# Two rows of a planner's table of durations: VectorE's searches and replacements, and activations into PSUM

## The chip, the cores and the metric

One core of one Trainium2 chip. The time is that of one execution on the device in microseconds, from which the median of three runs is given. The engines are TensorE (PE, with its weight loads PEld), VectorE (DVE), ScalarE (ACT), GpSimd (POOL) and SyncE (SP, which here issues DMAs).

## The reference

Top-k attention, and behind it two MLPs. Softmax runs over the 32 largest scores of each row alone.

```
B, H, S, D = 4, 8, 576, 64
scores = q @ k.T / sqrt(D);  kth = 32nd largest of each row
scores = where(scores >= kth, scores, -1e9);  attn = softmax(scores);  x = attn @ v      # x: 2304 x 512
h = x @ w_in;   g = 0 | (h+1)^2/4 | h  (h <= -1, between, h >= 1);   x = g @ w_out       # 512 -> 2048 -> 512
h = relu(x @ w_in2);   out = (h*h) @ w_out2
```

## The kernel before, in words

The 2304 rows of tokens form 18 token tiles T of 128 rows, and each has 8 heads, so there are 144 tiles of scores t = 8T + j. T = 4 and T = 13 hold rows of two batches, and each of their tiles takes two heads with 64 rows each. One tile of scores goes through:

- `scores`: 4 matmuls (8 in T = 4 and 13) into one of two PSUM areas, `s0` for even and `s1` for odd tiles
- `topk_ops`: on DVE four searches (`max`, the 8 largest of 576) and between them three replacements (`match_replace`, which blots out the 8 that were found; on the chip a MATCH_VALUE_LOAD and a MATCH_REPLACE8). The first search and the first replacement read `s`, the others the SBUF copy `W`. Each needs the one before it
- `below_` and `exp` on ACT, `exp_bias` (`nb`) on POOL, `prob_hi` on ACT and `prob_lo` on POOL (`pc`, high and low half in F16), `prob_trans` by a DMA on SP (`pT`)
- `attend`: 14 or 28 matmuls of `pT` with `vst` into an accumulator that shares PSUM tiles with the areas of scores

`below_` of tile t is the last reader of its area, so the scores of tile t+2 wait for it. `attend` shares banks with the area of the other parity and waits for DVE's reads of it.

Beside this run the preparation of k, v and q (`v_prep`: scaling on POOL or DVE, high half on ACT, rest on POOL or DVE; `q_scale`: a square sum `junk_q` on ACT, then `sc_q` and more on DVE), the decoding and splitting of the weights into `wall` in the first 270 us or so, and the MLPs in groups n of 24 matmuls: `h_n` into PSUM, then `mlp_act` (`r`, and in the first MLP a third activation that writes back into the PSUM tile `h`), `mlp_gate` on DVE, `mlp_split` (`g` or `gr`, ACT and POOL), and `o`. The room `xhl` is there once and is shared by `junk_q`, `qhl`, `hl_x`, `hl_y`.

What sets the order: `Book.note` takes down every operation with what it depends on and a key (the step at which it is due, less an urgency). `Book.order` then plays all of them through with durations from `Book.costs`: each engine takes, of the operations whose inputs would be there by then, the one with the smallest key. What comes out is written as the program, one in-order queue for each engine, with semaphores. `costs` gives two numbers: for how long the engine is taken, and when the result is there. Gaps in PE's queue while the weights are decoded, as the planner sees them, are filled with matmuls of `ones` (PLAN "warm", 15 to 300 us of its own time). All rows of the profile have line 400, where the operations are issued.

Of the kernel before, what the change touches and what calls it, by code (L numbers as in the profile page):

```python
# [143 lines left out]
class Book:  # L144
# [107 lines left out]
    def costs(self, engine, method, args, kwargs, outs, ins):  # L252
        views = [v for v in outs + ins if v.elements() > 8]
        n = max((v.elements() for v in outs), default=0)
        wide = any(v.tile.ring.psum for v in views)
        aps = sum(isinstance(a, View) and a.elements() == 1 for a in (*args[2:], kwargs.get("bias"), kwargs.get("scale"), kwargs.get("accum_out")))
        if engine == "PE":
            c = n * (4 if args[2].ap.dtype is F32 else 1) / 2400.0 + 0.0024
            return c, c + 0.16
        if method == "dma_start_transpose":  # L260
            return (1.33 if n < 1100 else 1.41), n * 256 / 1000 / 165
        if method == "dma_start":
            v = (outs + ins)[0]
            return 0.6, 4 * v.elements() * v.ap.ap[0][1] / 1000 / (210 if outs and len(v.ap.ap) > 2 else 420)
        if engine == "DVE":
            if method == "max":
                return 0.68, 0.75
            if method == "match_replace":
                return 0.76, 0.85
            c = 0.07 + (n if method != "tensor_reduce" else 128) / 960 + (0.05 if n > 64 else 0.0)  # L270
            return c, c + 0.08
        if engine == "ACT":
            c = 0.155 + n / 1400 - (0.03 if wide else 0.0) + 0.09 * aps - (0.04 if n < 300 else 0.0)
            return c, c + 0.1
        if method == "memset":
            return 0.07, 0.07
        c = 0.14 + n / 522 if method == "tensor_tensor" else 0.14 + n / 940 + (0.08 * aps if n < 8 else 0.0)
        if any(v.ap.dtype is U16 for v in ins):
            c += 0.1
        return c, c  # L280
# [1218 lines left out]
```

## Time and profile before

| | us |
|---|---|
| median of 3 runs | 1068.32 (1068.06 to 1068.46) |
| the profiled execution | 1068.74 |
| its span, first to last instruction | 1067.0 |
| PE busy | 1000.5 |
| DVE busy | 915.3 |
| ACT busy | 847.4 |
| POOL busy | 673.1 |

The granted TensorE clock was 0.995 of full speed over the span. Busy times are sums over stages that differ; which engine ends a stage is read from stretches and from the gaps in front of instructions (in square brackets: how long the engine had been idle, and what released it).

### The profile page before, as it was taken

The numbers are of one execution on the slowest core, as the hardware profiler recorded it, in microseconds if no ns is written. First come the engines' busy times: TensorE is split into PE (matmuls) and PEld (weight loads), VectorE is DVE, ScalarE is ACT, GpSimd is POOL, SyncE is SP. The second block draws the span as 40 slices with busy tenths as digits, with TensorE's granted clock in tenths as the row PEclk, the third lists the DMA queues.
The fourth block names the chain that finished last, engine by engine and source line by source line (L and its number), as shares of the span: only waits on it lengthen the run. The fifth ranks groups of instructions, "written<-read, shape, count | busy, mean of one in ns | idle before, by whom it ended". The sixth has DMA issues, their size and how long they took to land.

```text
span 1067.0 us, 24296 instructions
## 1 busy us (share of the span) xinstructions
PE 1000.5 (94%) x8576; PEld 560.1 (52%) x8576; DVE 915.3 (86%) x2053; ACT 847.4 (79%) x1538; POOL 673.1 (63%) x1052
## 2 busy tenths in 40 slices
PE   4867889899889999999999999999999999999998
PEld 3744567666567544544544545444445445454443
DVE  5999999999999999999999999999999999991100
ACT  4778999999678898878988797987878887775542
POOL 4696989999667574648776564667674646553221
PEclk9989999999999999999999999999999999999999
DMA  9999886755766687879988778789767676764333
GB/s 251 319 312 235 218 214 141 141 123 99 136 115 121 128 157 139 158 135 155 185 135 143 120 139 159 136 154 169 150 131 130 108 136 114 123 107 92 75 59 66
DMA packets 433834, 158.11 MB, mean 148 GB/s; under 512 B 412208, under 2 KB 419376, under 8 KB 433712
## 3 DMA queue, kind: packets, MB, share of 16 engines
q1 hardware_dynamic: 433712, 156.56, 72.9%
q8 instruction: 67, 1.10, 0.4%
q14 instruction: 55, 0.45, 0.1%
HBM read 55.31 MB, written 4.72 MB: 56 GB/s over the span
## 4 chain that ended last, share of the span: by engine, by line
PE 66%; ACT 9%; DVE 7%; DMA 6%; POOL 6%; issue 4%; SPq 1%; POOLq 0%; ACTq 0%; DVEq 0%
PE h L400 28%; PE o L400 28%; PE s L400 9%; DVE m L400 2%; DVE W L400 2%; ACT wall L400 2%; ACT W L400 2%; POOL wall L400 2%; DMA l_q<-in_q_dram 2%; POOL pc L400 1%; DMA pT<-pc 1%; SPq L400 1%; ACT r L400 1%; DMA wall<-in_moe_w_in_dram 1%; DMA l_v<-in_v_dram 1%
## 5 line engine op out<-in xcount | busy, mean ns | idle before, releaser
L400 PE MATMUL o<-wall,g 128*128 128x512 f16 x1728 | 430.4, 379 | 9.8 <-POOL g L400 3.8
L400 DVE MAX8 m<-W 128x8 f32<-128x576 f32 x432 | 323.7, 755 | 5.6
L400 PEld LDWEIGHTS <-g 128*128 128x128 f16 x1728 | 159.6, 98 | 188.5 <-issue 6.2
L400 POOL TENSOR_TENSOR pc<-W,pc 128x64 f16<-128x64 f32 (+1 forms) x288 | 205.3, 734 | 76.0 <-ACT pc L400 65.8
L400 POOL TENSOR_TENSOR gr<-r,gr 128x512 f16<-128x512 f32 x116 | 134.3, 1158 | 155.8 <-ACT gr L400 138.2
L400 DVE MATCH_REPLACE8 W<-m,W 128x576 f32<-128x576 f32 x288 | 213.9, 743 | 0.0
L400 PE MATMUL h<-wall,T_y 128*128 128x512 f16 x720 | 166.6, 379 | 0.0
L400 PE MATMUL h<-wall,T_x 128*128 128x512 f16 x672 | 156.3, 379 | 0.0
L400 ACT ACTIVATE W<-W,nb,esc 128x576 f32<-128x576 f32 x144 | 124.5, 865 | 13.8 <-POOL nb L400 9.9
L400 ACT ACTIVATE W<-s,m 128x576 f32<-128x576 f32 x144 | 105.9, 736 | 36.4 <-DVE m L400 22.6
L400 DVE MAX8 m<-s 128x8 f32<-128x576 f32 x144 | 109.1, 758 | 17.2 <-PE s L400 10.3
L400 PEld LDWEIGHTS <-wall 128*128 128x128 f16 (+1 forms) x1600 | 96.5, 98 | 43.2 <-DVE wall L400 11.1
L400 PEld LDWEIGHTS <-T_y 128*128 128x128 f16 x720 | 70.2, 98 | 83.8
L400 PE MATMUL s<-kst,qT 128*128 128x64 f16 (+3 forms) x640 | 96.0, 290 | 16.5 <-ACT W L400 16.0
L400 PEld LDWEIGHTS <-pT 128*128 128x128 f16 (+1 forms) x2240 | 83.9, 100 | 47.3 <-issue 11.7
L400 DVE MATCH_REPLACE8 W<-m,s 128x576 f32<-128x576 f32 x144 | 107.8, 749 | 0.0
L400 PEld LDWEIGHTS <-T_x 128*128 128x128 f16 x672 | 65.0, 98 | 76.8
L400 PE MATMUL s<-vst,pT 128*128 128x65 f16 (+1 forms) x2240 | 92.4, 194 | 10.1 <-DMA pT<-pc 5.3
L400 ACT ACTIVATE pc<-W 128x576 f16<-128x576 f32 x144 | 97.3, 677 | 2.0 <-DMA pT<-pc 0.7
L400 POOL TENSOR_SCALAR nb<-m,esc 128x1 f32<-128x1 f32 x144 | 53.3, 370 | 67.0 <-DVE m L400 57.5
L400 ACT ACTIVATE r<-r 128x512 f32<-128x512 f32 x144 | 90.5, 628 | 2.5
L400 ACT ACTIVATE r<-h,B,A 128x512 f32<-128x512 f32 x72 | 55.8, 774 | 38.0 <-PE h L400 38.0
(156 smaller groups left out, 1320.5 us busy)
## 6 DMA issues: line engine op xcount, KB each, us to landing
wall<-in_moe_w_in_dram SPq DMA_DIRECT2D x32, 512.0 KB, 6.6
wall<-in_moe_w_out_dram SPq DMA_DIRECT2D x30, 512.0 KB, 5.4
out_dram<-ob SPq DMA_DIRECT2D x18, 256.0 KB, 2.5
l_q<-in_q_dram SPq DMA_DIRECT2D x16, 256.0 KB, 3.8
n_v<-in_v_dram SPq DMA_DIRECT2D x24, 144.0 KB, 2.8
n_k<-in_k_dram SPq DMA_DIRECT2D x12, 288.0 KB, 3.0
l_k<-in_k_dram SPq DMA_DIRECT2D x12, 288.0 KB, 3.4
pT<-pc SPq DMA_TRANSPOSE x144, 3.4
```

The source lines that it names most:

```text
L400: op.fn(*(real(a) for a in op.args), **{k: real(a) for k, a in op.kwargs.items()})
```

## The change

For a search the planner now has 0.70 and 0.76 us (engine taken, result there) for 0.68 and 0.75; for a replacement 0.70 and 0.82 for 0.76 and 0.85. An activation whose output lies in PSUM gets 0.05 us more than one in SBUF; before, one that touched PSUM at either end got 0.03 less. So the third activation of `mlp_act` and the decoding into PSUM are 0.08 us longer in the table. Activations that only read PSUM keep their numbers. Everything else of the code is the same, and `order` is run anew with these numbers.

```diff
             if method == "max":
-                return 0.68, 0.75
+                return 0.7, 0.76
             if method == "match_replace":
-                return 0.76, 0.85
+                return 0.7, 0.82
...
-            c = 0.155 + n / 1400 - (0.03 if wide else 0.0) + 0.09 * aps - (0.04 if n < 300 else 0.0)
+            c = 0.155 + n / 1400 + (0.05 if outs and outs[0].tile.ring.psum else -0.03 if wide else 0.0) + 0.09 * aps - (0.04 if n < 300 else 0.0)
```

In the rows below, the first number behind m8 and W is the tile, the number at the end of a name the buffer (it differs between the two programs without meaning). First DVE at tiles 26 and 27, around the step `sc_q4` that needs the square sum of q tile 4. Before:

```order
L400 MAX m8_26_3723<-W_26_3745 128x8
L400 MAX m8_27_3776<-s1_234 128x8
L400 MATCH_REPLACE W_26_3745<-m8_26_3723,W_26_3745 128x576
L400 TENSOR_SCALAR wall_75<-wall_75,s_o2_3574 128x512
L400 MAX m8_26_3723<-W_26_3745 128x8
L400 MATCH_REPLACE W_27_3845<-m8_27_3776,s1_234 128x576
L400 MATCH_REPLACE W_26_3745<-m8_26_3723,W_26_3745 128x576
L400 TENSOR_SCALAR sc_q4_3861<-qn2_4_3850 128x1
```

And now:

```order
L400 MATCH_REPLACE W_26_3751<-m8_26_3741,W_26_3751 128x576
L400 MAX m8_27_3826<-s1_227 128x8
L400 MAX m8_26_3741<-W_26_3751 128x8
L400 TENSOR_SCALAR wall_75<-wall_75,s_o2_3632 128x512
L400 MATCH_REPLACE W_26_3751<-m8_26_3741,W_26_3751 128x576
L400 TENSOR_SCALAR wall_75<-wall_75,s_o2_3632 128x512
L400 MAX m8_26_3741<-W_26_3751 128x8
L400 TENSOR_SCALAR sc_q4_3896<-qn2_4_3871 128x1
L400 MATCH_REPLACE W_27_3901<-m8_27_3826,s1_227 128x576
```

The last search of tile 26 and one more scaling of `wall` have moved ahead of `sc_q4`, the first replacement of tile 27 behind it.

Next DVE at tiles 36 and 37, where PE's scores of tile 38 wait for the last search of tile 36. Before:

```order
L400 MAX m8_36_4939<-W_36_4968 128x8
L400 MAX m8_37_5063<-s1_234 128x8
L400 SCALAR_TENSOR_TENSOR vst_1_0_4869<-l_v_1_0_4903,sv_840,vst_1_0_4869 128x5x64
L400 MATCH_REPLACE W_36_4968<-m8_36_4939,W_36_4968 128x576
L400 TENSOR_SCALAR sc_y2_5095<-yn2_2_5078 128x1
L400 TENSOR_SCALAR AZ_1934<-AZ_1934,is_i2_2503 128x2
L400 MAX m8_36_4939<-W_36_4968 128x8
```

And now:

```order
L400 MAX m8_37_5072<-s1_227 128x8
L400 MATCH_REPLACE W_36_5041<-m8_36_5016,W_36_5041 128x576
L400 MATCH_REPLACE W_37_5103<-m8_37_5072,s1_227 128x576
L400 MAX m8_36_5016<-W_36_5041 128x8
L400 SCALAR_TENSOR_TENSOR vst_1_0_5019<-l_v_1_0_4899,sv_773,vst_1_0_5019 128x5x64
L400 MATCH_REPLACE W_36_5041<-m8_36_5016,W_36_5041 128x576
L400 MAX m8_37_5072<-W_37_5103 128x8
L400 TENSOR_SCALAR rs_4_5172<-s1_227 128x2
L400 MAX m8_36_5016<-W_36_5041 128x8
```

The first replacement and the second search of tile 37 have moved ahead of the last search of tile 36.

Last POOL at tile 113, where v of batch 3 is prepared (`l_v_3_7` is its head 7 as loaded, `vst_3_7` the result that the attend of tile 111 reads). Before:

```order
L400 TENSOR_TENSOR gr_99_12214<-r_99_12141,gr_99_12214 128x512
L400 TENSOR_SCALAR l_v_3_7_12125<-l_v_3_7_12125,sv_840 128x320
L400 TENSOR_TENSOR pc_113_12229<-W_113_12110,pc_113_12229 128x64
L400 TENSOR_TENSOR pc_113_12229<-W_113_12110,pc_113_12229 128x512
L400 TENSOR_TENSOR vst_3_7_11901<-l_v_3_7_12125,vst_3_7_11901 128x5x64
```

And now:

```order
L400 TENSOR_TENSOR gr_99_12241<-r_99_12175,gr_99_12241 128x512
L400 TENSOR_SCALAR l_v_3_6_12162<-l_v_3_6_12162,sv_773 128x320
L400 TENSOR_TENSOR pc_113_12263<-W_113_12145,pc_113_12263 128x64
L400 TENSOR_TENSOR pc_113_12263<-W_113_12145,pc_113_12263 128x512
L400 TENSOR_TENSOR vst_3_6_11925<-l_v_3_6_12162,vst_3_6_11925 128x5x64
L400 TENSOR_SCALAR l_v_3_7_12168<-l_v_3_7_12168,sv_773 128x320
L400 TENSOR_TENSOR gr_100_12295<-r_100_12275,gr_100_12295 128x512
L400 TENSOR_TENSOR vst_3_7_11931<-l_v_3_7_12168,vst_3_7_11931 128x5x64
```

Head 6 now stands behind `gr_99`, and head 7 has moved behind the pair for `pc_113` and the rest of head 6.

## Rows read from the trace of the kernel before

**Rows 1.** The page's part 1: busy us, share of the span, instructions.

```profile
PE 1000.5 (94%) x8576; PEld 560.1 (52%) x8576; DVE 915.3 (86%) x2053; ACT 847.4 (79%) x1538; POOL 673.1 (63%) x1052
```

**Rows 2.** Busy time by stretch: length, PE, PEld, DVE, ACT, POOL, clock, DMA, GB/s.

```profile
280.00:300.00 20.00, 14.78 (x227) 11.22 (x225) 19.96 (x49) 11.81 (x22) 11.57 (x33) 1.00 0.83 131
```

**Rows 3.** The same view, three long stretches behind it.

```profile
313.00:480.00 167.00, 166.89 (x1413) 92.75 (x1412) 162.02 (x379) 142.80 (x279) 96.28 (x147) 1.00 0.74 138
...
490.00:780.00 290.00, 289.86 (x2089) 141.00 (x2088) 275.42 (x596) 244.61 (x442) 190.93 (x315) 1.00 0.81 150
...
785.00:1050.00 265.00, 265.00 (x1662) 128.59 (x1660) 176.40 (x383) 186.01 (x313) 123.37 (x182) 1.00 0.59 104
```

**Rows 4.** Timeline of PE: start, us, instruction, count [idle before it <- releaser].

```profile
292.43 0.70 PE L400 MATMUL s<-kst,qT 128*64 128x64 f16 x8 [2.52 <-ACT W L400]
...
296.96 0.64 PE L400 MATMUL s<-vst,pT 128*64 128x65 f16 x28 [1.38 <-DVE m L400]
...
312.17 0.44 PE L400 MATMUL s<-vst,pT 128*64 128x65 f16 x16 [0.88 <-DVE W L400]
...
782.12 0.60 PE L400 MATMUL s<-vst,pT 128*64 128x65 f16 x14 [1.39 <-ACT vst L400]
...
783.68 0.57 PE L400 MATMUL s<-vst,pT 128*64 128x65 f16 x13 [0.21 <-POOL vst L400]
```

**Rows 5.** Timeline of DVE, tiles 35 to 38.

```profile
290.19 0.75 DVE L400 MAX8 m<-s 128x8 f32<-128x576 f32 x1
290.87 0.74 DVE L400 MAX8 m<-W 128x8 f32<-128x576 f32 x1
...
300.41 0.76 DVE L400 MAX8 m<-W 128x8 f32<-128x576 f32 x1
301.21 0.09 DVE L400 MATCH_VALUE_LOAD W<-m,W 128x8 f32 x1
301.29 0.74 DVE L400 MATCH_REPLACE8 W<-m,W 128x576 f32<-128x576 f32 x1
302.06 0.76 DVE L400 MAX8 m<-W 128x8 f32<-128x576 f32 x1
...
304.20 0.75 DVE L400 MATCH_REPLACE8 W<-m,s 128x576 f32<-128x576 f32 x1
304.86 1.41 DVE L400 MAX8 m<-W 128x8 f32<-128x576 f32 x2
```

**Rows 6.** Timelines of DVE, SP and ACT: two DVE waits, and the second one's origin.

```profile
101.99 0.09 DVE L400 MATCH_VALUE_LOAD W<-m,s 128x8 f32 x1 [1.62 <-PE s L400]
...
224.88 1.26 SPq L400 DMA_TRANSPOSE T_x<-hl_x  x1
...
229.79 0.63 ACT L400 ACTIVATE junk_q<-l_q 128x512 bf16<-128x512 f32 x1 [1.15 <-issue]
...
230.55 0.15 DVE L400 TENSOR_SCALAR sc_q<-qn 128x1 int32<-128x1 int32 x1 [2.17 <-ACT junk_q L400]
```

**Rows 7.** Timelines of PE and DVE: the scores and first search of tile 19.

```profile
165.23 0.65 PE L400 MATMUL s<-kst,qT 128*128 128x64 f16 x4 [0.52 <-ACT W L400]
...
168.57 0.76 DVE L400 MAX8 m<-s 128x8 f32<-128x576 f32 x1
```

**Rows 8.** Timelines of POOL and ACT at tile 113 (v of batch 3, head 7).

```profile
779.83 1.16 POOL L400 TENSOR_TENSOR gr<-r,gr 128x512 f16<-128x512 f32 x1 [1.67 <-ACT gr L400]
780.97 0.53 POOL L400 TENSOR_SCALAR l_v<-l_v,sv 128x320 f32<-128x320 f32 x1
781.47 1.42 POOL L400 TENSOR_TENSOR pc<-W,pc 128x64 f16<-128x64 f32 x2
...
781.61 0.46 ACT L400 ACTIVATE vst<-l_v 128x320 f16<-128x320 f32 x1
...
782.85 0.78 POOL L400 TENSOR_TENSOR vst<-l_v,vst 128x320 f16<-128x320 f32 x1
...
783.61 0.69 POOL L400 TENSOR_SCALAR l_q<-l_q,sq 128x512 f32<-128x512 f32 x1
```

**Rows 9.** Groups of instructions, shapes apart: busy us, mean ns | idle before them.

```profile
L400 ACT ACTIVATE r<-h,B,A 128x512 f32<-128x512 f32 x72 | 55.8, 774 | 38.0 <-PE h L400 38.0
...
L400 ACT ACTIVATE h<-h,NG,A 128x512 f32<-128x512 f32 x72 | 53.3, 741 | 0.0
```

## The prediction

> **What bounds the kernel now.** I read the stretches of time first, then the gaps in front of single instructions, then the two orders. TensorE (PE) is busy 1000.5 us, VectorE (DVE) 915.3 [rows 1]. In 280 to 300 us PE works 14.78 of 20 us while DVE works 19.96 [rows 2]: until then DVE, with the searches of the top-k, is the bound and PE waits for it. From 313 us on it is the other way round: PE works 166.89 of 167, 289.86 of 290 and 265.00 of 265 us [rows 3], and DVE has 5.0 and 14.6 us of rest in the first two of these. So the end is the time at which PE stops running out of work (312 us), plus the matmuls that are then left, plus the few gaps behind that. The last early gaps stand in front of the scores of tile 37 (2.52 us), the attends of tiles 34 and 36 (1.38, 0.88); the largest later one splits the attend of tile 111 (1.39 and 0.21) [rows 4]. (A tile here is 128 rows of scores. Its number follows from counting the searches that read `s`.)
>
> **What the change does.** No instruction is added or removed; PE alone gets 39 more of its filler matmuls (946 for 907), which stand only where the planner sees it idle in the first part. The planner's numbers are not waited for on the chip: engines start when their semaphores allow. So a number costs only by the order it makes. Counted in the two orders, 991 of DVE's 1623 operations stand at another place, by 3.6 places in the mean; PE's last tenth is nearly untouched, and behind the scores of tile 53, and of most tiles after it, exactly the same PE work is left in both. What counts is therefore what happens before 313 us, and each later place where an operand comes late.
>
> *Term 1, neighbours on DVE.* A search or replacement whose successor belongs to another tile lets it start 0.68 us later (290.19 to 290.87) or 0.66 (304.20 to 304.86). If the successor needs its result, it takes 0.80 (300.41 to 301.21) or 0.77 (301.29 to 302.06) [rows 5]. The difference is 0.11 to 0.12 us for each dependent pair that stands side by side. The old table charged 0.76 before something else may follow a replacement, the new one 0.70, nearer to its search; its planner sees less to gain from mixing two tiles. Counted in the orders: such pairs number 329 before and 363 now, and up to the last search of tile 36, where PE still waits for DVE, 20 before and 29 now. 9 x 0.11 = **+1.0 us** on DVE's front. (Up to tile 48 it is 15 more, 1.7; the rest lies where DVE has rest.)
>
> The Trainium skill (VectorE: DVE Perf Modes, The DRAIN you can't avoid) says that the next DVE operation does not start until the pipe is empty, and that leaving the semaphore out changes nothing. By that, neighbours would cost the same whether they depend or not, and term 1 would be 0. The rows above disagree here: the 0.75 us search at 290.19 is followed after 0.68.
>
> *Term 2, the longest DVE wait.* At 230.55 DVE has stood 2.17 us for the norm of q tile 4 (`junk_q`), which ACT could start only at 229.79, since the room it writes is held until the transpose of `hl_x`, issued at 224.88, has read it [rows 6]. In the new order DVE has more in front of that step (one more scaling of `wall` and the last search of tile 26, one replacement less; by the rows' durations 0.9 us over the whole list ahead of it), and POOL has 1.3 us less in front of the half of `hl_x` that the transpose waits for. Together that could take the whole wait; the first alone takes 0.9. I take the middle, **-1.5 us** (-2.2 to -0.9).
>
> *Term 3, a new DVE wait.* The first search of tile 19 ran at 168.57, long after its scores (165.23 plus 0.65) [rows 7]. It now has 3.2 us less DVE work in front, so it would be there at 165.4 and wait for scores that end at 165.9: **+0.5 us**. If the scores come later too (PE has 1.9 us more of real work in front of them, in place of 37 fillers) it is up to 2.4; if DVE is late by then, 0.
>
> These three give the front of DVE at tile 35: 1.0 - 1.5 + 0.5 = 0.0 us.
>
> *Term 4, tiles 36 to 39 against PE.* The new order runs tiles 36 and 37 side by side, so the last search of 36 comes behind one replacement (0.74) and one search (0.68) more, 1.4 us later. The scores of 38 wait for it. But PE has 1.1 us more MLP work in front of them, so 0.3 is lost. In return the replacement of tile 39 that the attend of 36 waited for (0.88 [rows 4]) comes nearly 2 us sooner, and that gap goes: 0.3 - 0.9, about **-0.5 us** (-0.9 to +0.4, where the 1.4 is only partly covered).
>
> *Term 5, the attend of tile 111.* Its second operand is `vst_3_7`. Before, POOL scaled its input at 780.97, right behind `gr`; ACT wrote the high half at 781.61, and PE went on at 782.12, 1.15 us after the scaling began [rows 4, 8]. Now POOL first scales `l_v_3_6`, then does the pair for `pc`, then the rest of `vst_3_6`: with 0.50, 1.38 and 0.76 us from start to start [rows 8] the scaling of `l_v_3_7` begins at 780.97 + 2.64 = 783.6 and PE goes on at 784.8. PE has 4 matmuls of `o` (0.9 us) moved ahead of this, arriving at 780.7 + 0.9 = 781.6. The gap is 3.2 us instead of 1.6, or 2.3 if `gr`, which has two activations fewer in front of it on ACT, starts up to 0.9 sooner. I take **+1.2 us** (+0.7 to +1.6; -1.6 if all is sooner, +2.6 if the whole 2.6 shift counts). PE has nothing spare behind that place, so it goes to the end in full.
>
> *The activations into PSUM.* These are 72 gates `h` and the decodes. The gate's activation into PSUM took 741 ns, the one from the same place into SBUF 774 [rows 9]; the new table has it 0.08 us longer than before. It moves consumers on DVE by a place or so, and while PE is the bound nobody on the chip waits for that: 0, and its cover is the rest of DVE named above.
>
> **The sum.** 0.0 - 0.5 + 1.2 = +0.7 us. The profiled execution took 1068.74 (span 1067.0, 1.7 around it), 0.4 above the median of 1068.32. The same shift on the median gives **1069.0 us**.
>
> **Rivals.**
> *DVE's front is late (slower).* The wait at 230.55 stays, because the transpose also comes later, and the neighbours up to tile 48 count: 1.7 + 0.5 = 2.2 on the front; with terms 4 and 5, +2.9, so 1071.2. For it speaks that DVE is full (19.96 of 20) [rows 2] just ahead of the place where PE runs dry; against it, that DVE had 2.17 and 1.62 us waits [rows 6] which a new order need not hit again. It decides from a front that is 1.4 us late.
> *DVE's waits go (faster).* The 2.17 at 230.55 and the 1.62 at 101.99 [rows 6] both vanish and tile 19 doesn't wait: 1.0 - 2.2 - 1.6 = -2.8, with terms 4 and 5 -2.1, so 1066.2. PE could follow, since it had 5.2 us of gaps in 280 to 300 [rows 2].
> *Nothing happens on the path.* The queue of PE falls back into the old one before any of it counts, tile 111 included: 1068.3.
> *Dependent neighbours cost nothing extra.* Then term 1 is 0 and the sum -0.3: 1068.0. This is the rule of the Trainium skill weighed under term 1 (VectorE: DVE Perf Modes, The DRAIN you can't avoid). The starts in rows 5 speak against it.
>
> **How the numbers follow.** The measurement can tell about 0.2% (2.1 us) from no change. Chances: forecast 0.35, nothing on the path 0.12, free neighbours 0.03 (all within 0.2%); late front 0.35; waits gone 0.15. So faster 0.15, same 0.50, slower 0.35. All lower bounds at once (1.0 - 2.2 - 0.9 - 1.6) give -3.7, all upper ones (1.7 - 0.9 + 2.4 + 0.4 + 2.6) +6.2; they hardly come together, and I keep two thirds: -2.4 to +4.2, from 1065.9 to 1072.5. The forecast's own range is 1067.5 to 1070.4.
>
> **What the profile after would show.** Term 1: more starts on DVE that are 0.77 to 0.80 us behind the row before them. Term 2: the wait of `sc_q` near 230 us under 1.3 us. Term 3: a wait of about 0.5 us before a first search near 165. Term 4: a gap before the scores of tile 38, none before the attend of 36. Term 5: a PE gap of 2.3 to 3.2 us near 782, put down to `vst`. I am wrong if PE runs dry again after 330 us, if the early gaps end more than 2 us from 312, or if `vst_3_7` is in time.

## The result and the profile after

The changed kernel takes 1079.2 us (median of 4 runs, 1078.79 to 1080.71) beside 1068.4 for the kernel before, measured along with it: the ratio is 1.0099, with a 95% interval of 1.0081 to 1.0117. The prediction was 1069.0 (1065.9 to 1072.5), so it was wrong: the change costs 10.8 us, and the time lies far outside the range. The profiled execution took 1078.79 us; its span is 1077.0, ten more than before.

The busy times (engine, us, share of the span, instructions) barely show it:

```profile
PE 1009.3 (94%) x8615; PEld 566.5 (53%) x8615; DVE 915.3 (85%) x2053; ACT 843.2 (78%) x1538; POOL 672.1 (62%) x1052
```

Against [rows 1] VectorE is busy for the same 915.3 us. TensorE has 8.8 us more, with the same work but for 39 more fillers; so part of its busy time is slower work (see the last section). The stretches tell where the time went. First 140 to 200 us of the kernel before, columns as in [rows 2]:

```profile
140.00:200.00 60.00, 52.48 (x685) 39.34 (x686) 57.19 (x130) 56.83 (x105) 54.40 (x72) 1.00 0.76 175
```

and the same and later stretches of the changed kernel:

```profile
140.00:200.00 60.00, 50.99 (x676) 38.97 (x674) 51.56 (x115) 54.49 (x96) 49.71 (x65) 1.00 0.67 162
220.00:240.00 20.00, 17.23 (x214) 13.01 (x213) 18.93 (x47) 18.54 (x38) 18.89 (x23) 0.91 0.77 151
280.00:300.00 20.00, 17.02 (x215) 11.10 (x213) 19.86 (x58) 13.48 (x24) 14.78 (x31) 0.95 0.73 116
313.00:480.00 167.00, 165.22 (x1429) 92.50 (x1427) 160.89 (x377) 140.90 (x277) 95.82 (x151) 1.00 0.72 134
490.00:780.00 290.00, 285.92 (x2052) 139.04 (x2049) 272.96 (x595) 239.74 (x438) 191.34 (x322) 1.00 0.81 148
785.00:1050.00 265.00, 265.00 (x1709) 128.89 (x1708) 186.94 (x406) 189.32 (x321) 128.74 (x191) 1.00 0.59 107
```

In 140 to 200 us VectorE works 5.6 us less than it did (51.56 for 57.19). From 313 to 480 and from 490 to 780 TensorE, which was full in [rows 3], now rests 1.8 and 4.1 us. Two losses, then: VectorE's searches come late early on, and TensorE runs dry after 330 us, which the prediction had named as the sign that it is wrong.

The first loss is on VectorE's timeline (start, us, instruction, [idle before it <- releaser]), changed kernel, tiles 16 to 20:

```profile
152.41 0.76 DVE L400 MAX8 m<-W 128x8 f32<-128x576 f32 x1
156.75 1.43 DVE L400 MAX8 m<-s 128x8 f32<-128x576 f32 x2 [3.58 <-PE s L400]
...
185.27 0.77 DVE L400 MAX8 m<-s 128x8 f32<-128x576 f32 x1 [1.53 <-PE s L400]
```

VectorE is through with tile 16 at 153.17 and then stands 3.58 us for the scores of tile 17, the next entry of its queue. What TensorE does meanwhile:

```profile
152.07 2.84 PE L400 MATMUL h<-T_x,wall 128*128 128x128 f16 x48
154.75 0.39 PE L400 MATMUL gram_o<-wall 128*128 128x128 bf16 x4
154.98 0.38 PE L400 MATMUL lo_o<-wall,neg 128*128 128x512 f16 x1
155.20 1.03 PE L400 MATMUL o<-wall,g 128*128 128x512 f16 x4
156.06 1.14 PE L400 MATMUL s<-kst,qT 128*128 128x64 f16 x8
```

The scores of tiles 17 and 18 stand side by side (x8) behind 48 matmuls of `h`. Before, the scores of 17 ran at 149.94, by themselves, and VectorE's longest wait near them was 0.41 us:

```profile
149.94 0.65 PE L400 MATMUL s<-kst,qT 128*128 128x64 f16 x4
...
153.72 0.77 DVE L400 MAX8 m<-s 128x8 f32<-128x576 f32 x1 [0.41 <-PE s L400]
```

By counting the searches, tile 16 begins at the same time in both kernels (143.2), tile 20 9.3 us later. The last search of tile 36 is 5.7 us late, that of tile 44 only 2.4, that of 64 8.0 and that of 143 9.7. Single tiles vary, since the new order mixes neighbouring tiles otherwise. TensorE's matmuls of the scores give a steadier measure. Here are those of tiles 40, 53, 80 and 143 (found by counting, as the searches were), before:

```profile
312.76 0.65 PE L400 MATMUL s<-kst,qT 128*128 128x64 f16 x4
...
395.18 0.65 PE L400 MATMUL s<-kst,qT 128*128 128x64 f16 x4
...
561.95 0.65 PE L400 MATMUL s<-kst,qT 128*128 128x64 f16 x4
...
952.88 0.65 PE L400 MATMUL s<-kst,qT 128*128 128x64 f16 x4
```

and after the change:

```profile
317.82 0.65 PE L400 MATMUL s<-kst,qT 128*128 128x64 f16 x4
...
401.62 0.65 PE L400 MATMUL s<-kst,qT 128*128 128x64 f16 x4
...
571.31 0.65 PE L400 MATMUL s<-kst,qT 128*128 128x64 f16 x4
...
962.71 0.65 PE L400 MATMUL s<-kst,qT 128*128 128x64 f16 x4
```

They come 5.1, 6.4, 9.4 and 9.8 us late, with as much matmul work left behind them as before (0.4 us less at tile 40). So about half of the loss is there when the early gaps end, and the other half arises later, most of it by tile 80.

The second loss, TensorE's gaps of the changed kernel:

```profile
229.90 1.12 PE L400 MATMUL s<-kst,qT 128*128 128x64 f16 x4 [2.48 <-ACT W L400]
...
297.41 0.82 PE L400 MATMUL s<-kst,qT 128*64 128x64 f16 x8 [2.16 <-ACT W L400]
...
384.25 0.44 PE L400 MATMUL s<-vst,pT 128*128 128x65 f16 x9 [0.81 <-DVE W L400]
...
529.88 0.65 PE L400 MATMUL s<-kst,qT 128*128 128x64 f16 x4 [0.58 <-ACT W L400]
...
532.14 5.34 PE L400 MATMUL o<-wall,g 128*128 128x512 f16 x24 [1.28 <-ACT ob L400]
...
779.60 2.10 PE L400 MATMUL o<-wall,g 128*128 128x512 f16 x9 [0.64 <-ACT ob L400]
```

None of them stands where [rows 4] had one but that of 297.41, which has its counterpart at 292.43.

### The profile page after: what moved, and what is told of

It is laid out like the page before. It is cut to its first block, busy times and chain, and to the rows that moved or that the text cites. A ratio compares the mean times of both kernels' runs of the same rounds, so it can differ in the third digit from the quotient of the medians.

```text
span 1077.0 us, 24373 instructions
## 1 busy us (share of the span) xinstructions
PE 1009.3 (94%) x8615; PEld 566.5 (53%) x8615; DVE 915.3 (85%) x2053; ACT 843.2 (78%) x1538; POOL 672.1 (62%) x1052
## 4 chain that ended last, share of the span: by engine, by line
PE 56%; ACT 12%; POOL 9%; DVE 9%; DMA 8%; issue 5%; SPq 2%; POOLq 0%; ACTq 0%; DVEq 0%
PE o L400 24%; PE h L400 24%; PE s L400 7%; DVE m L400 3%; POOL wall L400 3%; ACT W L400 3%; DVE W L400 3%; POOL pc L400 2%; DMA wall<-in_moe_w_in_dram 2%; ACT wall L400 2%; SPq L400 2%; ACT r L400 2%; ACT pc L400 1%; DMA wall<-in_v_dram 1%; DVE wall L400 1%
## 5 line engine op out<-in xcount | busy, mean ns | idle before, releaser
L400 PE MATMUL o<-wall,g 128*128 128x512 f16 x1728 | 428.8, 379 | 12.2 <-ACT g L400 4.1
L400 DVE MAX8 m<-s 128x8 f32<-128x576 f32 x144 | 108.9, 757 | 19.7 <-PE s L400 14.6
L400 PEld LDWEIGHTS <-wall 128*128 128x128 f16 (+1 forms) x1600 | 99.2, 101 | 50.0 <-DVE wall L400 18.5
```

The costliest lines, as they stand in the source:

```text
L400: op.fn(*(real(a) for a in op.args), **{k: real(a) for k, a in op.kwargs.items()})
```

## The experiments

The theories, in the order in which they came up:

- A: the new numbers of VectorE do the harm; B: the longer activations into PSUM do it.
- C: the steps in PLAN were fitted to one order, and any other order loses.
- D: the time follows the length of the planner's own timetable of an order. Every change of the table, however small, draws a new order; the old one happens to be short.
- E: the loss is made of a few single waits, and a wait that is mended comes back at the end; F: what one wait gives back the next one takes.

**One half of the change at a time (e1, e2).** The edits, e1 and then e2, each on the kernel before:

```diff
-                return 0.68, 0.75
+                return 0.7, 0.76
...
-                return 0.76, 0.85
+                return 0.7, 0.82
```

```diff
-            c = 0.155 + n / 1400 - (0.03 if wide else 0.0) + 0.09 * aps - (0.04 if n < 300 else 0.0)
+            c = 0.155 + n / 1400 + (0.05 if outs and outs[0].tile.ring.psum else -0.03 if wide else 0.0) + 0.09 * aps - (0.04 if n < 300 else 0.0)
```

> The kernel before with the two new pairs for searches and replacements alone; activations into PSUM keep the old numbers. Theory A (the numbers of VectorE do the harm: its searches are sent too early or too late against the preparation of the weights, so its front comes late by 6 us near 290 us, and TensorE with it): 1076 to 1080 us, the two long TensorE gaps near 230 and 297 us are there again. Theory B (the longer activations into PSUM do it): 1067 to 1070. Theory C (the other numbers of the plan were fitted to one order, and any other order loses some us, wherever the change is): 1071 to 1080, with gaps at other places than in the changed kernel.

> The kernel before with the longer activations into PSUM alone. Theory A: 1067 to 1070 us, as before. Theory B: 1076 to 1080. Theory C: 1071 to 1080. What the prediction said of this half is that it costs nothing (within 1 us of before).

Measured: VectorE's numbers alone 1075.83 us (ratio 1.0068, 1.0053 to 1.0083); PSUM's alone 1081.97 (1.0126, 1.0111 to 1.0141), more than both together. So neither A nor B by itself, and the halves don't add up (6.8 + 13.0 is not 10.8). Theory A had forecast 1076 to 1080 us for e1 with TensorE's gaps near 230 and 297 us again; neither gap is there. e2 lies above the 1080 us of both B and C. The half that the prediction had put down at zero is the dearer one. In e2 the gaps stand at other places again; its largest stands before the attend of tile 71:

```profile
534.40 0.61 PE L400 MATMUL s<-vst,pT 128*128 128x65 f16 x14 [4.14 <-DMA pT<-pc]
```

**A change that says nothing (e3).** The kernel before with

```diff
-                return 0.68, 0.75
+                return 0.681, 0.751
```

> The kernel before with 0.681 and 0.751 us for a search in place of 0.68 and 0.75: a thousandth of a us, which says nothing new of the hardware but has the order made anew. Theory A and Theory B: within 1.5 us of before (1067 to 1070), since no duration is wronger than it was. Theory C: 1071 to 1080, with a front of VectorE that is late and other late gaps.

Measured: 1068.31 us (0.9996, 0.9986 to 1.0006), no change, although 326 of VectorE's 1623 operations stand at another place. C in its strong form falls: an order made anew need not lose.

**The new table from tile 40 on (e4).** The kernel before, with the new numbers where `self.step` is at least 320:

```diff
-                return 0.68, 0.75
+                return (0.68, 0.75) if self.step < 320 else (0.7, 0.76)
...
-                return 0.76, 0.85
+                return (0.76, 0.85) if self.step < 320 else (0.7, 0.82)
...
-            c = 0.155 + n / 1400 - (0.03 if wide else 0.0) + 0.09 * aps - (0.04 if n < 300 else 0.0)
+            c = 0.155 + n / 1400 + ((0.05 if self.step >= 320 else -0.03) if outs and outs[0].tile.ring.psum else -0.03 if wide else 0.0) + 0.09 * aps - (0.04 if n < 300 else 0.0)
```

> The kernel before up to the operations that are due with tile 40, and the whole new table for those that are due from there on. If some 6 us of the loss arise in the first 320 us and some 4 in the gaps after it, as the two traces read, and the two are independent: 1071.5 to 1073.5 us, with TensorE's last early gap at 312 us as before. If the late gaps only follow from the early delay (the same work meets other transfers): 1067 to 1070. If the late part alone can do all of it: above 1075.

Measured: 1080.13 us (1.0110, 1.0094 to 1.0127), as much as the whole change, out of the late part alone. Up to 312 us its trace is that of before (the gap of [rows 4] at 312.17 is there at 311.44). Then TensorE runs dry while the last tiles of a token tile are still being searched:

```profile
361.70 1.04 PE L400 MATMUL o<-wall,g 128*128 128x512 f16 x4 [1.49 <-POOL g L400]
...
367.25 0.59 PE L400 MATMUL s<-vst,pT 128*128 128x65 f16 x14 [2.29 <-DVE m L400]
...
369.68 6.75 PE L400 MATMUL h<-wall,T_x 128*128 128x512 f16 x24 [0.58 <-DMA T_x<-hl_x]
```

and when it has work again, it has so much of it ahead of the next scores that VectorE stands still in its turn:

```profile
396.43 0.77 DVE L400 MAX8 m<-s 128x8 f32<-128x576 f32 x1 [5.88 <-PE s L400]
```

Tile 48 begins its last search 2.9 us sooner than in the kernel before, tile 52 6.7 us later: 9.6 us lost within four tiles. So the rest that VectorE has behind 313 us is no cover: here both engines are nearly full, first TensorE waits for VectorE and then VectorE for TensorE, and the time is lost to both.

**Theory D.** `Book.order` plays the order through and so has a timetable with a length of its own (`self.length`), which nothing in the program reads and which the prediction did not use. It is 1042.4 us long for the kernel before and 1051.1 for the changed one. The planner's times and the trace agree in where it is lost: the planner has the last search of tile 20 5.2 us late and that of 143 8.7 us, the trace 8.8 and 9.7; in e4 the planner's lateness goes from -3.6 at tile 48 to +6.1 at tile 52, the trace's from -2.9 to +6.7. Then I played through some 250 tables that differ from the old one by at most 0.003 us in five kinds of operations, and as many that so differ from the new one. Every one gave a longer timetable than the kernel before has: 1043.2 to 1063.8 us around the old table (median 1048.8), 1045.5 to 1065.5 around the new one (median 1051.5). So the kernel before is the best of its neighbourhood, and the changed kernel an ordinary member of its own. Four such orders went to the chip.

The edit of e5 (on the changed kernel), e6 and e7 (on the kernel before), with other thousandths in each:

```diff
-        op.cost = self.costs(engine, method, args, kwargs, outs, ins)
+        d, r = {"max": (0, -0.003), "match_replace": (-0.002, 0.003), "DVE": (0.002, -0.003), "ACT": (0, -0.001), "POOL": (0, 0.003)}.get(method if method in ("max", "match_replace") else "" if "dma" in method else engine, (0, 0))
+        busy, there = self.costs(engine, method, args, kwargs, outs, ins)
+        op.cost = busy + d, there + r
```

The edit of e8, on the kernel before, moves the table the other way:

```diff
-                return 0.68, 0.75
+                return 0.66, 0.74
...
-                return 0.76, 0.85
+                return 0.82, 0.88
...
-            c = 0.155 + n / 1400 - (0.03 if wide else 0.0) + 0.09 * aps - (0.04 if n < 300 else 0.0)
+            c = 0.155 + n / 1400 - (0.11 if outs and outs[0].tile.ring.psum else 0.03 if wide else 0.0) + 0.09 * aps - (0.04 if n < 300 else 0.0)
```

> The changed kernel, with thousandths of a us (at most 0.003) added to or taken from the planner's numbers of five kinds of operations. Played through by the planner its own timetable is 1045.5 us long; that of the changed kernel is 1051.1, that of the kernel before 1042.4. Theory D (what the time follows is the length of the timetable of that one order, which any new order draws anew; what the new numbers say of VectorE and of PSUM hardly matters): 5.6 us less than the changed kernel, so 1070 to 1075 us (the six kernels so far took 24.7 to 31.1 us more than their timetables). Theory A or B (the new numbers themselves do the harm): 1077 to 1081, as the changed kernel.

> The kernel before, its table changed by at most 0.003 us, with a timetable of 1051.1 us, as long as that of the changed kernel. Theory D: 1076 to 1082 us, as slow as the changed kernel although the table is the old one in all that matters. Theory A or B: 1067 to 1071, as before and as the nudge of one thousandth in the earlier run.

> The kernel before, its table changed by at most 0.003 us, with a timetable of 1063.8 us, the longest of some 250 such changes. Theory D: 1088 to 1095 us. Theory A or B: 1067 to 1071.

> The kernel before with its table moved the other way: 0.66 and 0.74 us for a search, 0.82 and 0.88 for a replacement, activations into PSUM 0.08 us shorter. Its timetable is 1054.8 us long. Theory A or B (the direction of the change does the harm): 1064 to 1070 us, no slower than before. Theory D: 1079 to 1086.

Measured: e5 1074.76 us (1.0054, 1.0036 to 1.0072), e6 1073.88 (1.0045, 1.0030 to 1.0061), e7 1090.85 (1.0207, 1.0186 to 1.0229), e8 1082.77 (1.0132, 1.0107 to 1.0156). Three thousandths of a microsecond in a table of durations cost 22 us in e7, twice what the change costs; the new table with as small a nudge loses 6 us instead of 11; and the opposite change loses more than the change itself. So the direction of the change does not decide, as A and B have it, and the forecasts from D hold for e5, e7 and e8. e6 fell short of what was expected (1076 at the least): with a timetable as long as the changed kernel's it is 5 us faster. The length tells the size only to some 4 us.

Part of that scatter is that each length is reckoned with its own table. If every order is kept as it came out, and only its times are played through again with the numbers of the old table, each engine taking its operations in the order written, the lengths are:

| kernel | own timetable | order replayed with the old numbers | measured |
|---|---|---|---|
| before | 1042.4 | 1041.8 | 1068.4 to 1069.2 |
| changed | 1051.1 | 1054.0 | 1079.2 |
| e1, VectorE's numbers | 1047.1 | 1050.5 | 1075.8 |
| e2, PSUM's numbers | 1057.3 | 1055.9 | 1082.0 |
| e3, one thousandth | 1043.4 | 1042.2 | 1068.3 |
| e4, new from tile 40 | 1049.0 | 1049.6 | 1080.1 |
| e5, new, nudged | 1045.5 | 1047.9 | 1074.8 |
| e6, old, nudged | 1051.1 | 1049.0 | 1073.9 |
| e7, old, nudged | 1063.8 | 1060.8 | 1090.9 |
| e8, opposite | 1054.8 | 1052.8 | 1082.8 |
| e12, new from tile 20 | 1043.3 | 1044.1 | 1068.7 |

The replay puts the changed order 12.2 us behind the old one at equal durations; measured it is 10.8. So the loss needs no effect of the chip: it is in which operation stands ahead of which. Measured less replayed is 24.6 to 30.5 us in all rows, and what is left of 3 us either way is not explained. The closeness of 12.2 and 10.8 is partly luck. How PSUM sharing is treated in the replay moves the 12.2 to as much as some 17, and with the new numbers in place of the old ones the changed order is only 5 to 6 us longer. It is longer in each of these replays, so the sign holds and the size only roughly.

Does the new table give longer orders in general, or did it only draw an unlucky one? Replays of some 250 neighbours of each table (in a reckoning that has 1041.6 and 1053.8 for the two kernels' orders) have their medians at 1047.8 for the old table and 1054.8 for the new one with the old numbers, and at 1049.1 and 1051.6 with the new numbers. So the old order is some 6 us shorter than an ordinary one of its own table, and orders of the new table are another 2.5 to 7 us longer. No run on the chip parts the two; e5 to e7 were chosen by their length. Why the old order is so short is open too. The steps in PLAN may have been chosen along with it, which is what is left of C; no run tests that.

**The new table from tile 20 on (e12).** The same edit as in e4, with 160 in place of 320.

> The new table for all operations that are due with tile 20 or later, the old one ahead of that. It holds the whole of the change that cost 11 us in the run with the new table from tile 40 on, and 20 tiles more. Its timetable is 1043.3 us long, 0.9 longer than that of the kernel before. Theory D (the length of the timetable tells it): 1066 to 1074 us. If the new numbers did harm behind tile 40 by what they are: 1078 or more.

Measured: 1068.67 us (0.9996, 0.9986 to 1.0005), as before. It holds everything that cost 11 us in e4 and 20 tiles more, and its short timetable had foretold 1066 to 1074. So behind tile 20 the new numbers need not cost anything: 619 operations of VectorE stand elsewhere, and nothing is lost.

**Mending single waits (e9 to e11).** The changed kernel, whose finished order is altered by hand. 1505 to 1508 are the scores of tile 17, 1163 is the first matmul of `h_1`; 2273 is the last search of tile 25 and 2295 its `below_`, 2243 the gate of `h_11`; 3396 and 3449 are the last replacement and search of tile 35, 3234 a step of `khl`. e9 has the first pair, e10 the other three, e11 all:

```diff
-        book.emit(book.order())
+        ops = book.order()
+        for ns, ahead in (((1505, 1506, 1507, 1508), 1163), ((2273,), 2243), ((2295,), 2243), ((3396, 3449), 3234)):
+            some = [op for op in ops if op.n in ns]
+            ops = [op for op in ops if op.n not in ns]
+            i = next(i for i, op in enumerate(ops) if op.n == ahead)
+            ops[i:i] = some
+        book.emit(ops)
```

> The changed kernel; in the order that comes out, the 4 matmuls of the scores of tile 17 are moved in front of the 48 matmuls of h (group 1), which stood ahead of them. In the changed kernel VectorE waited 3.58 us for these scores at 156.75 us; without the 48 and what follows them they would be there about 3 us sooner. Theory E (the loss is made of single waits like this one, and what is taken from one wait comes back at the end, since VectorE is full from there on): the wait falls to about 0.5 us and the time by 2 to 3 us against the changed kernel, 1076 to 1077.5. Theory F (what one wait gives back the next wait takes, since both engines are full and the order stays what it is): the wait falls, the time stays within 1 us of the changed kernel, 1078 to 1080.

> The changed kernel; on ScalarE the activation that frees the area of tile 25 is moved ahead of the gate h of group 11 and the high half of hl_x, and on VectorE the last replacement and search of tile 35 ahead of one scaling of khl and seven small steps for the constants. So TensorE's gaps of 2.48 us (at 229.90) and 2.16 us (at 297.41) should shrink to about 1.2 and 0.3 us. Behind each of the two the granted clock was 0.5 for 3.4 us; if the halves go as well, TensorE gets 1.7 us back at each place. Theory E with the clock: 3.1 + 3.4 = 6.5 us less than the changed kernel, 1072 to 1074. Theory E without the clock: 1075.5 to 1077. Theory F (VectorE is late anyhow and TensorE then waits for it at tiles 47 and 70): 1077.5 to 1080.

> The changed kernel with the moves of the two runs before this one together. Theory E: the sum of what the two gave back, down to 1069.5 to 1073 us if each gave what it could. Theory F: no more than the larger of the two, 1076 to 1080.

Measured: e9 1077.62 us (1.0087, 1.0072 to 1.0102), e10 1081.46 (1.0115, 1.0101 to 1.0129), e11 1081.19 (1.0119, 1.0102 to 1.0136). The changed kernel's interval is 1.0081 to 1.0117, so no gain is clear of the noise, and e10 and e11 are rather slower. e9 lies between the ranges of E (1076 to 1077.5) and F (1078 to 1080); e10 and e11 lie above those of both. The waits that were mended did go or shrink. In e9 VectorE (in an execution that is 1.9 us behind the changed kernel's when tile 16 begins):

```profile
154.77 0.76 DVE L400 MAX8 m<-W 128x8 f32<-128x576 f32 x1
155.45 0.75 DVE L400 MAX8 m<-s 128x8 f32<-128x576 f32 x1
159.24 0.77 DVE L400 MAX8 m<-s 128x8 f32<-128x576 f32 x1 [3.04 <-PE s L400]
```

The first search of tile 17 follows at once, with no wait; but the next entry of VectorE's queue is the first search of tile 18, whose scores are still behind the 48 matmuls, and it waits 3.04 us, while the replacement of tile 17, for which all is there, stands behind it. The last search of tile 17 has gained nothing by it: it is 2.2 us behind the changed kernel's. In e10 the gap of 2.48 us has shrunk to 1.28, the gap of 2.16 us at 297.41 is gone, and TensorE's next ones are

```profile
227.69 0.65 PE L400 MATMUL s<-kst,qT 128*128 128x64 f16 x4 [1.28 <-ACT W L400]
...
300.84 0.64 PE L400 MATMUL s<-vst,pT 128*64 128x65 f16 x28 [1.83 <-DVE W L400]
...
305.93 0.70 PE L400 MATMUL s<-kst,qT 128*64 128x64 f16 x8 [1.14 <-ACT W L400]
...
310.98 0.56 PE L400 MATMUL h<-T_x,wall 128*128 128x128 f16 x7 [2.09 <-DMA T_x<-hl_x]
```

So in e9 a queue that is fixed in order hands the wait on to its next entry, as F has it. In e10 and e11 more came back than was taken, which neither theory foresaw. A replay of their orders with the old numbers has it: e9's comes out 0.1 us shorter than the changed one, those of e10 and e11 2.6 and 2.5 us longer.

No version that beats the kernel before came out of this: no table tried by play-through has a shorter timetable than it, and the best two on the chip (e3, e12) only equal it.

## Why the prediction was wrong, point by point

- *"What counts is therefore what happens before 313 us, and each later place where an operand comes late."* This is the first step that failed: behind 313 us the sum has term 5 alone. TensorE being full in [rows 3] was read as a sign that VectorE, which has rest there, may be late without cost. VectorE was busy 162.02 of 167 and 275.42 of 290 us in the same rows: it was nearly full as well, and 5.0 and 14.6 us of rest are spread over some 73 tiles. Measured, the scores are 5.1 us late at tile 40 and 9.8 at tile 143, so nearly half of the loss arose behind 313 us. e4 shows it by itself: an order that is the old one up to 312 us loses 11 us behind it.
- *"1.0 - 1.5 + 0.5 = 0.0 us", the front of VectorE at tile 35.* This is the second step that failed. It sums places that could be seen in the trace of before. The terms were sized at waits that were there (230.55, 312.17, 782.12). A new order takes waits away where they were, and puts others where none was; the 3.58 us at tile 17 stood in no term, and the only new wait that was looked for was that of tile 19, at +0.5. The last search of tile 35 came 4.9 us late, that of tile 36 5.7.
- *Term 1, dependent neighbours, +1.0.* Right. Matched with the two orders, the second of a dependent pair starts 0.77 to 0.80 us behind the first in both traces, and 0.67 us is the median where it needs nothing of the first. Of such pairs there are 29 for 20 up to tile 36, 363 for 329 in all, so the term is 1.0 us, as predicted. It is a tenth of what was lost.
- *Term 2, the wait of `sc_q4`, -1.5.* Right in its place: at 238.18 `sc_q` starts with no wait before it, so all of the 2.17 us went (the upper end of what was given). It gained nothing, since VectorE was 7.6 us late there.
- *Term 3, tile 19, +0.5.* The first search of 19 had no wait; tile 17 had 3.58 and tile 20 1.53. Two tiles off, and 3.58 us in place of 0.5.
- *Term 4, tiles 36 to 39, -0.5.* The gap of 0.88 us before the attend of 36 went, as predicted, and there is none before the scores of 38. The gap before the scores of 37 stayed (2.16 for 2.52).
- *Term 5, tile 111, +1.2.* Wrong: `vst_3_7` comes late as predicted (POOL starts the scaling of `l_v_3_7` at 793.31, 1.4 us behind the start of the attend at 791.92; before, it was 0.5 us), but behind the 13 matmuls of the attend's first part the new order has 2 of `o` and 8 of `h`, 2.3 us (793.56 to 795.83), which cover it. The prediction counted only what had moved ahead of the attend, not what now stands inside it:

```profile
793.31 0.53 POOL L400 TENSOR_SCALAR l_v<-l_v,sv 128x320 f32<-128x320 f32 x1 [0.56 <-DMA l_v<-in_v_dram]
...
793.56 0.61 PE L400 MATMUL o<-wall,g 128*128 128x512 f16 x2
794.01 1.89 PE L400 MATMUL h<-wall,T_y 128*128 128x512 f16 x8
795.83 0.63 PE L400 MATMUL s<-vst,pT 128*64 128x65 f16 x14
```

- *The activations into PSUM, 0.* Wrong as well. On the chip nothing got longer by it: the gate takes 740 ns in the mean, 741 before [rows 9]. But the table is what the order is drawn from, and e2 alone cost 13 us.
- *The rival "VectorE's front is late"* had the right sign and the right place; its 1071.2 was too low, since it took the front's lateness for 2.2 us where 5.7 came (tile 36), and let little be lost behind it.
- *The range.* It was made from the ends of the terms (two thirds of -3.7 and +6.2 are -2.5 and +4.1, not -2.4 and +4.2; nothing hangs on it). The spread that mattered was that of orders: one to three thousandths in the table move the time by 0 to 22 us (e3, e6, e7), and of some 250 such orders none has a shorter timetable than the old one. With a kernel that is the best of its neighbourhood the likely result of any new draw is slower.

The rule that was weighed under term 1 was taken up only in part. The same paragraph (the Trainium skill, VectorE: DVE Perf Modes, The DRAIN you can't avoid) ends with "A next op that is not held starts earlier", so it does not make all neighbours cost the same. The trace shows such an earlier start: in e9 the independent search follows one of 0.76 us after 0.68 us (154.77 to 155.45).

## What to carry to other kernels

Where a change reaches the code through a planner, read the new order as a new draw: ask how the old one was chosen, play both through with the same durations (the old numbers and then the new), and take the spread of the orders from tiny changes of the table as the uncertainty, before any single wait is costed. Two engines that are both about 95% busy or more and feed each other have little cover to hide lateness behind, whichever of them is at 100%: here the scores of no tile from 53 on started less than 5 us late. A wait mended at one place in fixed queues was worth nothing here (e9), since the entry behind it could not start either.

## What was not expected of the hardware

Behind each of the two long TensorE gaps of the changed kernel the granted clock was at its lower level (1.2 of 2.4 GHz) for some 3.5 us (the first: 0.91 in the mean of 220 to 240 us, 0.09 x 20 / 0.5 = 3.6), where the kernel before had it at 1.00 even behind a gap of 2.52 us [rows 2, 4]. What it costs is seen in e10 and e11, whose orders are alike there: 36 matmuls of `h` behind a gap of 0.78 us, first e10, then e11.

```profile
229.12 3.69 PE L400 MATMUL h<-T_y,wall 128*128 128x128 f16 x36 [0.78 <-DVE r L400]
```

```profile
230.15 2.18 PE L400 MATMUL h<-T_y,wall 128*128 128x128 f16 x36 [0.78 <-DVE r L400]
```

The stretch 220 to 240 us of each (clock behind POOL's column):

```profile
220.00:240.00 20.00, 17.77 (x210) 13.49 (x211) 18.36 (x46) 18.68 (x39) 18.98 (x24) 0.91 0.75 138
```

```profile
220.00:240.00 20.00, 16.65 (x219) 12.20 (x220) 18.51 (x45) 18.83 (x38) 18.77 (x23) 1.00 0.77 152
```

So a fall costs 1.5 us at its place. Little of it is left soon after: the next attend begins 6.26 us behind the start of these matmuls in e10 (at 235.38) and 6.03 us in e11 (at 236.18), with the same matmuls in between, since e11 then waits for ScalarE and GpSimd (0.17 and 0.89 us). The clock does not explain the result either. Over the whole span, executions of the changed kernel had 0.988 to 0.992 and took 1078.79 to 1080.71 us; executions of the kernel before with the same 0.989 to 0.992 took 1067.0 to 1071.3 us. Why a gap of this size brings a fall in one execution and none in another stays open.
